# Running the FFN products of a fused attention and FFN kernel as pairs on the two column halves of the array, from the last of batch 1's transposes to the last kv

## Chip, cores, metric

One core of a Trainium2 chip. The metric is the device time of the core in microseconds, median of several executions. The record marks each execution as fast or slow (slow ones show a lower granted TensorE clock).

## The reference, cut to what matters

```python
def _attn_ref(q, k, v, g_norm):                  # 8 batches, 8 heads, 576 tokens, head size 64
    kv  = np.einsum('bhsd,bhse->bhde', k, v)     # 64 x 64 per head
    out = np.einsum('bhsd,bhde->bhse', q, kv)
    rms = np.sqrt(np.mean(out * out, axis=-1, keepdims=True) + 1e-06)
    return (out / rms * g_norm)

def _moe_ref(x, w_a, w_b, w_out):                # x: 4608 tokens x 512; d_ff 1536
    return ((x @ w_a) * (x @ w_b)) @ w_out
```

The attention's output, heads side by side, is the x of the FFN.

## The kernel before

TensorE does FFN products nearly all of the time, in nine strips of 512 tokens. The attention of the next batches is slipped in between. Three kinds of products divide the array differently:

- FFN products use all of it, 128 rows and 128 columns (128\*128 in the profile).
- `kv` gives each of two heads a column half (128\*64, or 96\*64 for the first batches), so two products run side by side. The transposes `qtr` do the same.
- `tx`, the token products of batches 2 to 7, give each head a row half (64\*128).

```python
    def product(o, lhsT, rhs, halves=False, **kw):
        for r in (slice(0, D), slice(D, 2 * D)) if halves else (slice(0, 2 * D),):
            nc.tensor.matmul(o[r], lhsT=lhsT[:, r], rhs=rhs, **kw)

        def kv(self, p, o):                       # class Attn
            ...
            for c, n in enumerate(rows):
                for j in range(2):
                    nc.tensor.matmul(
                        o[j * D : (j + 1) * D, :],
                        lhsT=kk[0:n, 2 * p + j, c, :],
                        rhs=vv[0:n, 2 * p + j, c, :],
                        start=(c == 0), stop=(c == len(rows) - 1))

        def tx(self, lent):                       # class Attn
            ...
                        r = slice(j * D, (j + 1) * D)
                        nc.tensor.matmul(
                            P[:, i, c0 + p * D : c0 + (p + 1) * D],
                            lhsT=self.qT[r, p, t0 : t0 + 128], rhs=self.kvs[r, p, :],
                            start=True, stop=True)

        def mm(self, w, kcs):                     # class Unit: one of 12 column blocks of d_ff
            t0 = self.s * STRIP
            for kc in kcs:
                nc.tensor.matmul(
                    self.a if w is wa_t else self.b,
                    lhsT=w[:, kc, self.fc * 128 : (self.fc + 1) * 128],
                    rhs=xt[:, kc, t0 : t0 + STRIP],
                    start=(kc == KORD[0]), stop=(kc == KORD[-1]))

    pieces = [(1, h1), (1, h2), (2, h1), (2, h2), (3, h1), (3, h2)]
    for n, (g, fcs) in enumerate(pieces):         # end of strip 0, with batch 1's attention
        halves = 0 < n < NP                       # NP = 4
        o_mm(0, g, O, fcs, halves=halves)         # six output products
        ...
        if n < NP:
            A.qtr(n, 2)
            A.kv1(n, 2)
        ...
    def slot(A, s, n):                            # called between the units of strip s
        k0, x0 = {1: (5, 6.5), 2: (1, 2.5), 3: (4, 5.5), 4: (0, 0.5), 5: (4, 5.5), 6: (0, 0.5)}[s]
        if n == k0 and s in (1, 2, 3, 5):
            two = [A] if s < 3 else [A, Attn(s + 2)]
            for i, a in enumerate(two):
                for p in range(NP):
                    a.kv(p, kb[:, i, p, :])       # 40 products a batch
            ...
        m = n - x0
        if m == 0:
            A.tx(ab_bank())                       # 40 products
```

So already before, pieces 1 to 3, which alternate with transposes and kv, were done in halves. The rest of the FFN was not.

Of the kernel before, what the change touches and what calls it, by code (L numbers as in the profile page):

```python
# [15 lines left out]
def kernel(  # L16
# [11 lines left out]
    nc = tc.nc  # L28

    B, H, S, D = q.shape  # L30
    d_model = H * D
# [4 lines left out]
    NP = H // 2  # L36
    HF = S // 2
    STRIP = 512
# [10 lines left out]
    def sb(shape, dt, name):  # L49
        return pool.tile(shape, dt, name=name, tag=name)  # L50
# [20 lines left out]
    xt = sb([128, KC, n_tok], BF16, "xt")  # L71
    abt = [[sb([128, STRIP], BF16, f"ab{i}_{f}") for f in range(FC)] for i in range(2)]
    a_sb = [sb([128, STRIP], BF16, f"asb{i}") for i in range(4)]
    sq = [sb([128, 2, HF], BF16, f"sq{i}") for i in range(3)]
# [16 lines left out]
    ones = sb([128, 128], BF16, "ones")  # L91
# [16 lines left out]
    P = psum.tile([128, 8, STRIP], FP32, name="P", tag="P")  # L108
    O = 3
# [44 lines left out]
        nc.sync.dma_start_transpose(qT[b % 2], qs_d[b])  # L154


    def product(o, lhsT, rhs, halves=False, **kw):
        for r in (slice(0, D), slice(D, 2 * D)) if halves else (slice(0, 2 * D),):
            nc.tensor.matmul(o[r], lhsT=lhsT[:, r], rhs=rhs, **kw)  # L159


    class Attn:
# [59 lines left out]
        def psq(self, p, i0):  # L222
            nc.scalar.activation(sq[p % 3], P[:, i0 : i0 + 2, 0:HF], AF.Square)

        def pss(self, p, i0, hs=(0, 1), halves=False):
            for h in hs:
                product(
                    P[:, i0 + h, 0:HF], ones, sq[p % 3][:, h, :], halves, start=True, stop=True
                )
            h0, h1 = hs[0], hs[-1] + 1  # L230
            nc.scalar.activation(  # L231
                rs[p % 3][:, h0:h1, :],
                P[:, i0 + h0 : i0 + h1, 0:HF],
                AF.Abs_reciprocal_sqrt,
                bias=eps_t,
            )
# [11 lines left out]
                )  # L248


        def x(self, p, i0, halves=False):
            for h in range(2):
                product(
                    P[:, i0 + h, 0:HF],
                    kvb[:, p, :],
                    self.qT[:, p, h * HF : (h + 1) * HF],
                    halves,
                    start=True,
                    stop=True,
                )  # L260
# [86 lines left out]
    class Unit:  # L347
        n = 0
# [6 lines left out]
        def mm(self, w, kcs):  # L355
            t0 = self.s * STRIP
            for kc in kcs:
                nc.tensor.matmul(  # L358
                    self.a if w is wa_t else self.b,
                    lhsT=w[:, kc, self.fc * 128 : (self.fc + 1) * 128],  # L360
                    rhs=xt[:, kc, t0 : t0 + STRIP],
                    start=(kc == KORD[0]),
                    stop=(kc == KORD[-1]),
                )
# [19 lines left out]
    def ab_bank():  # L384
        ab_banks.append(ab_banks.pop(0))
        return ab_banks[-1]
# [23 lines left out]

    n_o = [0]

    def o_mm(s, g, i, fcs, e0=0, e1=d_model, halves=False):
        for fc in fcs:
            product(
                P[:, i, e0:e1],
                abt[s % 2][fc][:, g * 128 : (g + 1) * 128],
                wo_t[:, fc, e0:e1],
                halves,
                start=(fc == 0),  # L420
                stop=(fc == FC - 1),
            )

    def o_out(s, g, i):
        n = n_o[0]
        n_o[0] += 1
        t = o_sb[n % 4]
        if n % 2:
            nc.scalar.copy(t, P[:, i, :])  # L429
        else:  # L430
            nc.vector.tensor_copy(t, P[:, i, :])  # L431
        store(s * STRIP + g * 128, t, 0, d_model)

    def ffn_o(s, g, i=O, between=None):
        o_mm(s, g, i, range(FC // 2))
        if between:
            between()
        o_mm(s, g, i, range(FC // 2, FC))
        o_out(s, g, i)
# [46 lines left out]
    X, SS = (4, 0), 6  # L486


    A = Attn(0)
# [14 lines left out]
    for c in range(EC):  # L504
        nc.tensor.matmul(
            P[:, SS, 0 : 2 * D],
            lhsT=kc0[:, c, :],
            rhs=vc[:, c, :],
            start=(c == 0),
            stop=(c == EC - 1),  # L510
        )
    for j in range(2):
        r = slice(j * D, (j + 1) * D)
# [7 lines left out]
    for p in range(1, NP):  # L521
        i = X[p % 2]
# [44 lines left out]
    A = Attn(1)  # L567
# [6 lines left out]
    pieces = [(1, h1), (1, h2), (2, h1), (2, h2), (3, h1), (3, h2)]  # L574
    for n, (g, fcs) in enumerate(pieces):

        halves = 0 < n < NP
        o_mm(0, g, O, fcs, halves=halves)
        if fcs is h2:
            o_out(0, g, O)  # L580
        if 0 <= n - 2 < NP:
            A.pss(n - 2, SS, halves=halves)
            A.pst(n - 2, X[n % 2])
        if 0 <= n - 1 < NP:
            A.x(n - 1, X[(n - 1) % 2], halves)
            A.psq(n - 1, X[(n - 1) % 2])
        if n < NP:
            A.qtr(n, 2)
            A.kv1(n, 2)
            A.kv_out(n, P[:, 2, STRIP - D :])  # L590
            A.qtr_out(n, 2)
# [9 lines left out]
    def slot(A, s, n):  # L601

        kb = P[:, 7, :].rearrange("q (b p e) -> q b p e", b=2, e=D)
        if s == 1:
            k0, xs = 5, (6.5, 8, 9.5, 11, 12.5)
        else:
            k0, x0 = {2: (2, 3.5), 3: (4, 5.5), 4: (0, 1.5), 5: (4, 5.5), 6: (0, 1.5)}[s]
            xs = tuple(x0 + x for x in (0, 1.5, 2.5, 4, 5))

        k0, x0 = {1: (5, 6.5), 2: (1, 2.5), 3: (4, 5.5), 4: (0, 0.5), 5: (4, 5.5), 6: (0, 0.5)}[s]  # L610
        if n == k0 and s in (1, 2, 3, 5):
            two = [A] if s < 3 else [A, Attn(s + 2)]
            for i, a in enumerate(two):
                for p in range(NP):
                    a.kv(p, kb[:, i, p, :])
            for i, a in enumerate(two):
                (nc.scalar.copy if i else nc.vector.tensor_copy)(a.kvs, kb[:, i])
        m = n - x0
        if m == 0:
            A.tx(ab_bank())  # L620
        for c in range(LC + 1):
            if m == 1.5 * c:
                A.tsq(c)
            if m == (1, 2, 4, 5, 7)[c]:
                A.tss(c)
            if m == (1, 2, 4, 5, 7)[c] + 0.5:
                A.trs(c)
            if m == (1, 2, 4, 5, 7)[c] + 1.5:
                A.txt(c)

    for s in range(1, N_STRIP - 1):
        b = s + 1
        A = Attn(b) if b < B else None
        for n in range(FC + 4):
            amid = (lambda n=n: slot(A, s, n - 0.5)) if A else None
            if n >= FC:
                ffn_o(s, n - FC, ab_bank() if n % 2 else O, amid)
            elif s > 1 or n > 1:
                ffn_ab(s, n, amid)
            if A:  # L640
                slot(A, s, n)

            if s == 1 and n == 3:
                load_late(3)
            if b + 1 < B and n == (12, 4, 8, 5, 8)[s - 1]:
                transpose_q(b + 1)
            if b + 2 < B and n == (14, 10, 14, 8)[s - 1]:
                load_late(b + 2)
# [12 lines left out]
    for i, copy, eng in ((6, nc.vector.tensor_copy, nc.sync), (7, nc.scalar.copy, nc.scalar)):  # L661
        e0 = hw + (i - 6) * qw
# [33 lines left out]
```

## Time and profile before

| | before |
|---|---|
| time, median (range) of the first 3 runs | 313.35 us (313.3 to 313.46) |
| span of the profile | 311.5 us |
| TensorE busy | 306.4 us, 98%, 2067 products recorded |
| full products of 512 columns, start to start | 215.8 ns |
| kv blocks between FFN products (128\*64) | 4: strips 1, 2, 3, 5 |
| tx blocks (64\*128) | 6: strips 1 to 6 |

Busy time is the union of intervals, so a pair that runs side by side counts once. A product's length (379 ns) is a latency. The pace is the distance between starts, which the timeline gives through the start of each next group. The lines themselves stand in the prediction.

### The profile page before, as it was taken

The page shows a single profiled execution, that of the slowest core. Times are in us where ns is not written, and L with a number is a line of the kernel's source. Part 1 is how long each engine was busy: PE and PEld are TensorE (multiplying, and loading weights), DVE is VectorE, ACT ScalarE, POOL GpSimd, SP SyncE. Part 2 cuts the span into 40 slices and gives each one's busy share as a digit, 9 for nine tenths or more (in the row PEclk, how much of TensorE's full clock was granted, in tenths as well). Part 3 has the DMA queues.
Part 4 walks back from the last instruction along what each step waited for, and adds up shares of the span by engine and source line. Part 5 has one row for each costly group of instructions (what it writes and reads, how often), then busy time and mean ns, then how long its engine had stood idle before and what let it go on. Part 6 is the DMA issues. An engine that isn't in the chain of part 4 may idle for free.

```text
span 311.5 us, 5288 instructions
## 1 busy us (share of the span) xinstructions
PE 306.4 (98%) x2067; PEld 145.7 (47%) x2067; DVE 140.7 (45%) x235; ACT 117.0 (38%) x231; POOL 101.2 (32%) x123
## 2 busy tenths in 40 slices
PE   8999999999999999999999999999999999999996
PEld 3444474444454444544444445444444444444444
DVE  4544335458238603484386123752783134213421
ACT  3643255354255313561554033632651233123310
POOL 8944991193274640043646300221240000000000
PEclk9999999999999999999999999999999999999999
DMA  8999999999799699046997980073021200030012
GB/s 180 197 196 199 200 189 161 223 133 165 169 172 177 106 198 168 2 89 126 172 185 109 185 167 2 19 160 109 20 51 42 103 1 0 36 100 1 0 36 101
DMA packets 94398, 36.21 MB, mean 116 GB/s; under 512 B 64934, under 2 KB 89894, under 8 KB 94374
## 3 DMA queue, kind: packets, MB, share of 16 engines
q0 software_dynamic: 59120, 18.44, 54.3%
q1 hardware_dynamic: 34786, 16.93, 23.8%
q10 hardware_dynamic: 468, 0.51, 0.6%
q8 instruction: 16, 0.26, 0.4%
q14 instruction: 8, 0.07, 0.1%
HBM read 37.78 MB, written 12.98 MB: 163 GB/s over the span
## 4 chain that ended last, share of the span: by engine, by line
PE 86%; DMA 7%; POOL 5%; issue 1%; ACT 0%; POOLq 0%
PE P L358 54%; PE P L159 29%; DMA wb_t<-in_moe_w_b_dram 6%; DMA vt<-in_v_dram 2%; PE P L176 2%; PE P L292 1%; POOL qt L119 1%; POOL wo_t L134 1%; POOL kt L119 1%; POOL vt L119 1%; POOL wb_t L477 0%; POOL wa_t L477 0%; POOL wa_t L130 0%; PE P L200 0%; POOL ident masks.py:199 0%
## 5 line engine op out<-in xcount | busy, mean ns | idle before, releaser
L376 DVE TENSOR_TENSOR ab<-P,asb 128x512 bf16<-128x512 f32 x108 | 74.5, 691 | 103.5 <-PE P L358 100.1
L358 PE MATMUL P<-xt,wa_t 128*128 128x512 bf16 x432 | 111.5, 379 | 0.1
L358 PE MATMUL P<-xt,wb_t 128*128 128x512 bf16 x432 | 111.3, 379 | 0.0
L372 ACT CAST asb<-P 128x512 bf16<-128x512 f32 x108 | 63.1, 586 | 90.0 <-PE P L358 90.0
L159 PE MATMUL P<-wo_t,ab 128*128 128x512 bf16 (+3 forms) x474 | 95.7, 368 | 0.0
L159 PEld LDWEIGHTS <-ab 128*128 128x128 bf16 (+1 forms) x474 | 44.0, 99 | 48.3
L358 PEld LDWEIGHTS <-wa_t 128*128 128x128 bf16 x432 | 41.8, 98 | 50.3 <-issue 0.6
L358 PEld LDWEIGHTS <-wb_t 128*128 128x128 bf16 x432 | 41.8, 98 | 49.8
L329 POOL TENSOR_TENSOR sqt<-rst,g_all 128x512 f32<-128x512 f32 (+1 forms) x24 | 25.0, 1043 | 84.7 <-ACT rst L322 84.7
L429 ACT COPY osb<-P 128x512 f32<-128x512 f32 x17 | 10.0, 586 | 70.2 <-PE P L159 65.6
L431 DVE COPY osb<-P 128x512 f32<-128x512 f32 x18 | 12.5, 692 | 44.9 <-PE P L159 44.9
L142 POOL DMA_DIRECT2D qs<-in_q_dram x12 | 19.8, 1654 | 0.7 <-issue 0.3
L313 DVE TENSOR_REDUCE sst<-sqt 128x8 f32<-128x512 f32 (+1 forms) x24 | 16.3, 680 | 1.7 <-ACT sqt L309 1.5
L338 DVE TENSOR_TENSOR qv<-P,sqt 128x512 bf16<-128x512 f32 x18 | 12.3, 681 | 0.0
L329 POOL TENSOR_TENSOR k_x<-rst,g_all 128x512 f32<-128x512 f32 x6 | 6.3, 1043 | 18.0 <-ACT rst L322 18.0
L322 ACT ACTIVATE rst<-sst,eps_t 128x8 f32<-128x8 f32 (+1 forms) x30 | 9.0, 300 | 7.0 <-DVE sst L313 6.8
L309 ACT ACTIVATE sqt<-P 128x512 f32<-128x512 f32 x18 | 10.5, 585 | 0.1
L241 DVE SCALAR_TENSOR_TENSOR xt<-P,g_col,rs 128x288 bf16<-128x288 f32 x16 | 7.5, 512 | 5.2 <-ACT rs L231 5.2
L134 POOL DMA_DIRECT2D wo_t<-in_moe_w_out_dram x12 | 6.4, 530 | 6.7 <-DMA wb_t<-in_moe_w_b_dram 3.1
L444 PE MATMUL P<-zeros 128*128 128x512 bf16 x17 | 6.6, 529 | 1.2 <-DVE eps_t L461 1.2
L231 ACT ACTIVATE rs<-P,eps_t 128x576 f32<-128x576 f32 (+1 forms) x9 | 6.1, 689 | 3.8 <-PE P L159 3.5
L139 POOL COPY gate<-qT 1x1 bf16<-1x1 bf16 x5 | 0.9, 176 | 17.3 <-DMA qT<-qs 17.2
(72 smaller groups left out, 130.8 us busy)
## 6 DMA issues: line engine op xcount, KB each, us to landing
out_dram<-osb SPq DMA_DIRECT2D x23, 256.0 KB, 2.0
qs<-in_q_dram POOLq DMA_DIRECT2D x12, 288.0 KB, 6.9
ktl<-in_k_dram POOLq DMA_DIRECT2D x6, 512.0 KB, 8.7
vtl<-in_v_dram POOLq DMA_DIRECT2D x6, 512.0 KB, 11.0
out_dram<-osb SPq DMA_DIRECT2D x13, 128.0 KB, 2.4
wo_t<-in_moe_w_out_dram POOLq DMA_DIRECT2D x12, 128.0 KB, 6.0
wa_t<-in_moe_w_a_dram POOLq DMA_DIRECT2D x5, 256.0 KB, 9.2
wb_t<-in_moe_w_b_dram POOLq DMA_DIRECT2D x5, 256.0 KB, 9.8
```

Of the source, the lines that this page charges most:

```text
L134: nc.gpsimd.dma_start(out=wo_t[:, i, :], in_=wo_v[:, i, :])
L142: nc.gpsimd.dma_start(out=d[:, hs, :], in_=q[b, hs].rearrange("h t d -> t h d"))
L159: nc.tensor.matmul(o[r], lhsT=lhsT[:, r], rhs=rhs, **kw)
L309: nc.scalar.activation(sqt[c % 3][r], self.by_head(c)[r], AF.Square)
L313: nc.vector.reduce_sum(sst[c % 3][r], sqt[c % 3][r].rearrange("t j p d -> t (j p) d"), axis=mybir.AxisListType.X,)
L329: nc.gpsimd.tensor_mul(sqt[c % 3][r].rearrange("t j p d -> t (j p) d"), rst[c % 3][r].unsqueeze(2).to_broadcast([n, H, D]), g_all[r].unsqu ...
L338: nc.vector.tensor_mul(t[r].rearrange("t (p j) d -> t j p d", j=2), self.by_head(c)[r], sqt[c % 3][r])
L358: nc.tensor.matmul(self.a if w is wa_t else self.b, lhsT=w[:, kc, self.fc * 128 : (self.fc + 1) * 128], rhs=xt[:, kc, t0 : t0 + STRIP], st ...
L372: nc.scalar.copy(self.t, self.a)
L376: nc.vector.tensor_mul(abt[self.s % 2][self.fc], self.b, self.t)
L429: nc.scalar.copy(t, P[:, i, :])
L431: nc.vector.tensor_copy(t, P[:, i, :])
```

## The change

Its intent: kv and FFN products use the same division of the array, so that nothing has to be switched around a kv. The flag becomes a state that stays on from piece 1 until just before the last kv (strip 5), and the products of `Unit.mm` go through `product` as well.

```diff
+    halves = [False]
-    def product(o, lhsT, rhs, halves=False, **kw):
-        for r in (slice(0, D), slice(D, 2 * D)) if halves else (slice(0, 2 * D),):
+    def product(o, lhsT, rhs, **kw):
+        for r in (slice(0, D), slice(D, 2 * D)) if halves[0] else (slice(0, 2 * D),):
             nc.tensor.matmul(o[r], lhsT=lhsT[:, r], rhs=rhs, **kw)
 ...                                     # pss, x, o_mm lose their own argument
         def mm(self, w, kcs):
             for kc in kcs:
-                nc.tensor.matmul(
+                product(
 ...
-        halves = 0 < n < NP
-        o_mm(0, g, O, fcs, halves=halves)
+        halves[0] = n > 0
+        o_mm(0, g, O, fcs)
 ...
         if n == k0 and s in (1, 2, 3, 5):
+            halves[0] = s < 5
```

More of the change, by code (lines that the diff above doesn't have):

```diff
@@ L223, in psq, with pss @@
             nc.scalar.activation(sq[p % 3], P[:, i0 : i0 + 2, 0:HF], AF.Square)
-        def pss(self, p, i0, hs=(0, 1), halves=False):
+        def pss(self, p, i0, hs=(0, 1)):
             for h in hs:
                 product(
-                    P[:, i0 + h, 0:HF], ones, sq[p % 3][:, h, :], halves, start=True, stop=True
+                    P[:, i0 + h, 0:HF], ones, sq[p % 3][:, h, :], start=True, stop=True
                 )
@@ L248, in pst, with x @@
                 )
-        def x(self, p, i0, halves=False):
+        def x(self, p, i0):
             for h in range(2):
@@ L256, in x @@
                     self.qT[:, p, h * HF : (h + 1) * HF],
-                    halves,
                     start=True,
@@ L357, in mm @@
             for kc in kcs:
-                nc.tensor.matmul(
+                product(
                     self.a if w is wa_t else self.b,
-                    lhsT=w[:, kc, self.fc * 128 : (self.fc + 1) * 128],
-                    rhs=xt[:, kc, t0 : t0 + STRIP],
+                    w[:, kc, self.fc * 128 : (self.fc + 1) * 128],
+                    xt[:, kc, t0 : t0 + STRIP],
                     start=(kc == KORD[0]),
@@ L411, with o_mm @@
     n_o = [0]
-    def o_mm(s, g, i, fcs, e0=0, e1=d_model, halves=False):
+    def o_mm(s, g, i, fcs, e0=0, e1=d_model):
         for fc in fcs:
@@ L418, in o_mm @@
                 wo_t[:, fc, e0:e1],
-                halves,
                 start=(fc == 0),
@@ L581 @@
         if 0 <= n - 2 < NP:
-            A.pss(n - 2, SS, halves=halves)
+            A.pss(n - 2, SS)
             A.pst(n - 2, X[n % 2])
         if 0 <= n - 1 < NP:
-            A.x(n - 1, X[(n - 1) % 2], halves)
+            A.x(n - 1, X[(n - 1) % 2])
             A.psq(n - 1, X[(n - 1) % 2])
```

## The prediction

> **What bounds the kernel now.** I read the page first: the line of busy times, then the chain that ended last.
>
> ```profile
> PE 306.4 (98%) x2067; PEld 145.7 (47%) x2067; DVE 140.7 (45%) x235; ACT 117.0 (38%) x231; POOL 101.2 (32%) x123
> PE 86%; DMA 7%; POOL 5%; issue 1%; ACT 0%; POOLq 0%
> ```
>
> TensorE is busy all the time, and after the loads of the start it is the whole chain. Busy is no proof of full pace, so I looked at its waits: the view of waits holds three for PE, 1.2, 0.4 and 0.2 us, all of the first 17 us. After that the end is set by how fast TensorE gets through its list, and only what changes that pace matters. Next, the matmul groups with shapes kept apart:
>
> ```profile
> L358 PE MATMUL P<-xt,wa_t 128*128 128x512 bf16 x432 | 111.5, 379 | 0.1
> L358 PE MATMUL P<-xt,wb_t 128*128 128x512 bf16 x432 | 111.3, 379 | 0.0
> L159 PE MATMUL P<-wo_t,ab 128*128 128x512 bf16 x402 | 88.6, 379 | 0.0
> L176 PE MATMUL P<-vtl,ktl 128*64 128x64 bf16 x240 | 4.6, 197 | 0.0
> L292 PE MATMUL P<-kvs,qT 64*128 64x64 bf16 x240 | 4.5, 190 | 0.0
> L159 PE MATMUL P<-wo_t,ab 128*64 128x512 bf16 x36 | 4.5, 379 | 0.0
> ```
>
> 128\*128 is the part of the array that a product uses (rows\*columns). Some 1,270 full products of 512 columns are the kernel. Their 379 ns is a latency; start to start the trace gives a mean of 215.8 ns. The kernel before already has 36 half products (128\*64), the kind that the change multiplies, so both cost and gain can be read from it. The timeline of TensorE around pieces 1 to 3 (start, length to the last end, group):
>
> ```profile
> 39.85 1.49 PE L159 MATMUL P<-wo_t,ab 128*64 128x512 bf16 x12
> 41.15 0.44 PE L159 MATMUL P<-qT,kvb 128*64 128x288 bf16 x4
> ...
> 44.14 0.38 PE L176 MATMUL P<-vt,kt 96*64 96x64 bf16 x12
> 44.33 1.49 PE L159 MATMUL P<-wo_t,ab 128*64 128x512 bf16 x12
> ...
> 46.80 1.47 PE L159 MATMUL P<-wo_t,ab 128*128 128x512 bf16 x6
> 48.10 0.41 PE L159 MATMUL P<-sq,ones 128*128 128x288 bf16 x2
> ```
>
> Twelve halves take from 39.85 to 41.15, 1.30 us; the six full products of the same work take from 46.80 to 48.10, also 1.30 us. A half pair costs what one full product costs. The timeline around the kv and the token products (tx) of strip 1:
>
> ```profile
> 59.63 1.03 PE L358 MATMUL P<-xt,wb_t 128*128 128x512 bf16 x4
> 60.59 0.82 PE L176 MATMUL P<-vtl,ktl 128*64 128x64 bf16 x40
> 61.34 1.04 PE L358 MATMUL P<-xt,wa_t 128*128 128x512 bf16 x4
> 62.22 1.03 PE L358 MATMUL P<-xt,wb_t 128*128 128x512 bf16 x4
> 63.08 1.03 PE L358 MATMUL P<-xt,wa_t 128*128 128x512 bf16 x4
> 64.04 0.76 PE L292 MATMUL P<-kvs,qT 64*128 64x64 bf16 x40
> 64.73 1.04 PE L358 MATMUL P<-xt,wb_t 128*128 128x512 bf16 x4
> ```
>
> Four full products from 59.63 end their pace at 60.49 (4 x 0.2158), but kv starts at 60.59: 0.10 us are lost at this change of the array's division. It is lost again at 61.34, at 64.04 and at 64.73, but not between 62.22 and 63.08 (0.86 = 4 x 0.2158).
>
> **What the Trainium skill says.** "TensorEngine Tiling (Array Packing)", Key Properties: changing the tiling mode, not just the tile, drains TensorE, and different tiles load weights and multiply independently. The trace agrees with both: about 0.10 us at each change of mode, and two halves in the time of one full product. The same page, Feature Incompatibilities, says that column tiling excludes Fast Weight Load. The load groups agree in direction (128\*64 takes 110 ns, 128\*128 takes 98 ns, for half the columns), but loads lie under the products. "TensorE: Matmul & The Clock Gate", Wait — 56ns, not 53.3ns?, gives N / 2.4 + 2.5 ns from start to start, 215.8 for N = 512; the 215.8 of the trace agrees. If the fixed 2.5 ns were paid per half, a pair would take 218.3; the half pairs of the trace start 215.5 ns apart inside a block, so it isn't.
>
> **The change part by part.**
>
> 1. *More instructions.* The instruction order of both kernels shows 4133 against 5401 rows on TensorE, a weight load and a product each: 634 further products. By hand: 12 + 6 in pieces 4 and 5 (output, norm and x products), 16 in the first units of strip 1, 80 + 48 for the rest of strip 1, 3 x 144 for strips 2 to 4, 40 for the units 0 to 4 of strip 5; 634. The order on VectorE, ScalarE, GpSimd and SyncE is the same. Price: 634 pairs x (215.5 - 215.8 ns), about 0; I count 0 and leave up to -0.2 us in the range.
>
> 2. *Switches removed.* Strips 1, 2, 3 and 5 hold a kv block, and before each has a switch in and one out. In, per instruction of the trace: 309 ns from the last full product to the first of kv instead of 216 (+93), and the second pair comes after 53 instead of the usual 32 ns (+21): 114 ns. Out: from the first of the last kv pair to the full product 131 instead of 32 (+99), and the second full product after 227 (+11): 110 ns. The chain shows the +11 and the drain together: 12 full products after a kv take 2.70 there, and 2.59 where no switch precedes them.
>
> ```profile
> 61.41 2.70 PE P L358 x12
> 149.13 2.59 PE P L358 x12
> ```
>
> Now halves hold from piece 1 until the last kv (strip 5). Removed: the four switches in, the switches out of strips 1, 2 and 3, and the one out after piece 3 (46.80); the one after strip 5's kv stays. 4 x 114 + 4 x 110 = 896 ns.
>
> 3. *Seams in their place.* Between kv and halves the pieces show 3 ns (44.33), then a first pair of 221 instead of 216. About 10 ns each way: 4 x 10 = 40 ns back.
>
> 4. *The tx blocks stay switched.* tx uses 64\*128, neither mode, so strips 1 to 4 still drain twice each, now from and to 128\*64. Before, in is 312 against 216 (+96), out 123 against 29 (+94) and +11. From columns halved the trace has only other cases (transposes 96\*64 to 64\*64 near 10 us: 136 against 39, +97), so a drain costs about the same. But of a half pair the second starts 3 to 28 ns after the first, so a drain may end later by that, and the first load without the fast path is longer (+21 against +11). Estimate 4 x 25 = 100 ns lost.
>
> Sum: -896 + 40 + 100 = -756 ns. All of it lies on the chain, as TensorE waits for nothing here. 313.35 - 0.75 = 312.6 us.
>
> **The rivals.**
>
> - *Halves are slower in long streams than in blocks of 12.* Double instruction traffic, double moving reads, no fast weight load. With the 2.5 ns per product of the skill, 634 x 2.5 = 1.6 us, net 314.2; at 10 ns it would be +6.3, net 318.9. Against it: 215.5 ns within all three blocks, while DMA was at its busiest, and kv blocks put a pair with two loads through every 32 ns, so loads and issue have room for seven times that rate. The instruction queue moved only 0.26 MB, and would move about 0.34 (x 5401 / 4133).
> - *tx switches get dearer when rows and columns change both.* Eight switches at 0.1 us more would eat the gain, 313.4. For it: no such switch is in the trace. Against: the five kinds there all cost 93 to 99 ns before refilling, whichever sides change.
> - *A load takes the place of the switch.* In strip 3 the second batch's values land at 124.16, and its products begin at about 124.97. TensorE would come some 0.6 us earlier, so the margin shrinks to 0.2; the issues (from 107.45) are held by earlier work that moves forward too. At worst 0.2 us lost, 312.8. In strip 1 the last values land at 59.32, 1.27 us ahead.
> - *Evictions.* A bank is full up to 28 ns later. PE waits for no eviction before, and VectorE and ScalarE are under half busy: nothing.
>
> **Range and chances.** The centre is 312.6. Full recovery with faster pairs gives 312.2; dearer tx switches or 1 ns per pair, up to 313.4. I take 312.1 to 313.5. The 2% lines are at 307.1 and 319.6: nothing removed reaches the first, and the second needs 10 ns a pair. Faster 0.01, within 2% 0.97, slower 0.02.
>
> **What would show it.** 2701 products; half pairs start 215 to 216 ns apart in long strips (by groups of four products: 0.86 us); kv blocks of strips 1 to 3 without the 0.10 us before and after; 0.10 us still at every tx and after the kv of strip 5; no new PE wait; span shorter by 0.6 to 0.9 us. I am wrong if pairs in long streams take over 217 ns, if PE's tx gaps exceed 0.15 us, or if a DMA releases kv.

## The result, and the profile after

The changed kernel took 312.68 us (312.43 to 313.0, 4 runs), the kernel before 313.38 us in the same rounds. The ratio is 0.9978, 95% interval 0.9961 to 0.9996. Ratios here are the mean time of one kernel's fast runs over that of the other's of the same rounds, so not quite the ratio of the medians. The interval lies below 1 as a whole. The gain is 0.70 us where 0.75 was forecast.

That agreement hides something. First the page of the changed kernel:

```profile
PE 304.3 (98%) x2684; PEld 157.6 (51%) x2701; DVE 140.6 (45%) x235; ACT 117.0 (38%) x231; POOL 101.3 (33%) x123
PE 79%; DMA 12%; POOL 7%; issue 1%; ACT 0%; POOLq 0%
```

There are 2701 weight loads, as predicted (17 records of their products are missing). But DMA's share of the chain rose from 7% to 12%. The timeline of TensorE after piece 3 and in strip 2 (start, length to the last end, group):

```profile
46.42 0.38 PE L178 MATMUL P<-vt,kt 96*64 96x64 bf16 x12
46.61 1.49 PE L161 MATMUL P<-wo_t,ab 128*64 128x512 bf16 x12
47.91 0.44 PE L161 MATMUL P<-sq,ones 128*64 128x288 bf16 x4
```

```profile
85.34 1.03 PE L161 MATMUL P<-xt,wb_t 128*64 128x512 bf16 x8
86.20 0.80 PE L178 MATMUL P<-vtl,ktl 128*64 128x64 bf16 x40
86.83 1.03 PE L161 MATMUL P<-xt,wa_t 128*64 128x512 bf16 x8
...
89.53 0.76 PE L293 MATMUL P<-kvs,qT 64*128 64x64 bf16 x40
90.21 1.05 PE L161 MATMUL P<-xt,wb_t 128*64 128x512 bf16 x8
```

The way out after piece 3 is gone: the FFN products start 0.19 us after the first kv product (46.61 - 46.42), where the kernel before took 0.31 us (46.80 - 46.49). In strip 2 everything is as intended. Eight halves take 86.20 - 85.34 = 0.86 us, the pace of four full products, and kv follows without a gap. kv takes 86.83 - 86.20 = 0.63 us, where the kernel before needed 61.34 - 60.49 = 0.85 for the same 40 products with a switch on either side. Strip 1 is different:

```profile
59.45 1.06 PE L161 MATMUL P<-xt,wb_t 128*64 128x512 bf16 x8
60.32 1.07 PE L178 MATMUL P<-vtl,ktl 128*64 128x64 bf16 x40
61.19 1.06 PE L161 MATMUL P<-xt,wa_t 128*64 128x512 bf16 x8
```

Here the 40 products take 61.19 - 60.32 = 0.87 us instead of 0.63. The chain that ended last (start, length, what) says why:

```profile
47.20 13.45 DMA vtl<-in_v_dram
60.69 0.69 PE P L178 x32
61.38 2.59 PE P L161 x24
```

After eight products kv waits for batch 2's last values, which land at 60.65 us. The kernel before had them at 59.32. So the wait that the prediction had placed in strip 3 came in strip 1, and took about 0.25 us (a gap of 251 ns where 29 is usual, and some 20 ns to get back into step).

The time of a run also scatters with its first 46 us, which are the same program in most of these kernels. In the profiles, piece 3's kv starts anywhere from 46.4 to 46.8 us without any change ahead of it (the three kernels with a changed start, at the end, are left aside). That is half of the gain. Therefore I use, beside the times, **the stretch**: from the last kv product of piece 3 to the start of the very last product of TensorE, as the trace has them. Two profiles of the kernel before agree on it to 1 ns (261.583 and 261.584 us). In the changed kernel it is shorter by 578 ns, with the wait in it.

### The profile page after: what moved, and what is told of

It reads as the page before. It is cut to its first block, busy times and chain, and to the rows that moved or that the text cites. A ratio compares the mean times of both kernels' runs of the same rounds, so it can differ in the third digit from the quotient of the medians.

```text
span 310.8 us, 6542 instructions
## 1 busy us (share of the span) xinstructions
PE 304.3 (98%) x2684; PEld 157.6 (51%) x2701; DVE 140.6 (45%) x235; ACT 117.0 (38%) x231; POOL 101.3 (33%) x123
## 4 chain that ended last, share of the span: by engine, by line
PE 79%; DMA 12%; POOL 7%; issue 1%; ACT 0%; POOLq 0%
PE P L161 77%; DMA wb_t<-in_moe_w_b_dram 6%; DMA vtl<-in_v_dram 4%; DMA wo_t<-in_moe_w_out_dram 2%; PE P L293 1%; PE P L178 1%; POOL vt L119 1%; POOL qt L119 1%; POOL qs L142 1%; POOL kt L119 1%; POOL wa_t L477 0%; POOL wb_t L477 0%; POOL wo_t L134 0%; POOL ktl L145 0%; POOL vtl L145 0%
## 5 line engine op out<-in xcount | busy, mean ns | idle before, releaser
L161 PE MATMUL P<-xt,wb_t 128*64 128x512 bf16 (+1 forms) x641 | 111.4, 379 | 0.2
L161 PE MATMUL P<-xt,wa_t 128*64 128x512 bf16 (+1 forms) x636 | 111.0, 379 | 0.6 <-issue 0.2
L161 PE MATMUL P<-wo_t,ab 128*64 128x512 bf16 (+3 forms) x673 | 95.5, 371 | 0.3
L161 PEld LDWEIGHTS <-ab 128*64 128x64 bf16 (+1 forms) x678 | 47.5, 106 | 45.0
L161 PEld LDWEIGHTS <-wa_t 128*64 128x64 bf16 (+1 forms) x644 | 46.0, 106 | 46.2 <-issue 0.6
L161 PEld LDWEIGHTS <-wb_t 128*64 128x64 bf16 (+1 forms) x644 | 45.8, 106 | 45.8
L444 PE MATMUL P<-zeros 128*128 128x512 bf16 x16 | 5.8, 510 | 1.2 <-DVE eps_t L461 1.2
```

## The experiments

All use the kernel before or the changed kernel with one edit, and all gave correct results. They ran in four groups; the time of before is that of the same group.

| kernel | time, us (before) | stretch against before, ns |
|---|---|---|
| changed, first profile | 312.68 (313.38) | -578 |
| after_again | 312.56 (313.32) | -725 |
| kv_later | 312.59 (313.32) | -824 |
| to_end | 312.50 (313.32) | -883 |
| price | 313.56 (313.32) | +226 |
| split_before | 314.48 (313.39) | +897 |
| split_after | 312.49 (313.39) | -821 |
| split_n | 315.02 (313.39) | +1584 |
| end_later | 312.21 (313.39) | -898 |
| shift_after | 313.22 (313.28) | -822 |
| shift_before | 313.90 (313.28) | -2 |
| before_again | 313.42 (313.28) | +1 |
| fetch_full | 313.72 (313.30) | -2 |

**Theories.** Mine: pairs cost nothing, each switch costs 0.11 us, and a load that varies eats part of the gain. Rivals: the halves are themselves faster or slower in long streams; kv is slow for another reason than the switch; the halves slow the DMAs.

### after_again: the changed kernel once more

> The changed kernel again. Median 312.5 to 312.8, spread wider than before's (some 0.5 us). Theory of the varying load wait: TensorE's wait inside the kv block of strip 1 (0.22 us in the first profile) is another length or gone in this profile, and the time differs accordingly. Rival, halves slow the DMA queues: the queues' shares are again 56% and 25% (before: 54.3% and 23.8%), with the landing of batch 2's last values after 60.4 again.

Measured: 312.56 us (312.44 to 312.96), ratio 0.9974 (0.9962 to 0.9987). The wait was there again but shorter: a gap of 105 ns inside kv, and a stretch of -725 instead of -578 ns. The wait thus varies from run to run. The DMA shares were 55.8% and 25.7% again, and the values landed at 60.61. So the later landing is no chance of one profile, and the rival about the DMAs stayed alive.

### kv_later: strip 1's kv half a unit later

```diff
-        k0, x0 = {1: (5, 6.5), 2: (1, 2.5), ...
+        k0, x0 = {1: (5.5, 6.5), 2: (1, 2.5), ...
```

> The changed kernel with strip 1's kv block half a unit (0.86 us) later. If the wait for batch 2's values is what keeps the gain under 0.80 us and makes it scatter: 312.5 to 312.6, spread back to 0.2 us or less, no gap inside the kv block of strip 1. If the scatter has another cause: the same 312.4 to 313.0 as the changed kernel.

```profile
60.38 1.06 PE L161 MATMUL P<-xt,wa_t 128*64 128x512 bf16 x8
61.24 0.82 PE L178 MATMUL P<-vtl,ktl 128*64 128x64 bf16 x40
61.87 1.06 PE L161 MATMUL P<-xt,wb_t 128*64 128x512 bf16 x8
```

kv takes 0.63 us in strip 1 too, the wait is gone, and the stretch is -824 ns. The times do not show it: 312.59 us (312.44 to 312.88) against the 312.56 of the changed kernel. The half of the expectation that spoke of the scatter failed: 0.44 us is left of it, so most of it does not come from this wait. The start is the likely place of what is left; the runs without a profile cannot show it.

### price: halves where no kv is

Halves only in strip 7 and in strip 8 but its last group, on top of the kernel before (pieces 1 to 3 as before).

```diff
     for s in range(1, N_STRIP - 1):
+        halves[0] = s == 7
```

> The kernel before with halves in strip 7 and all of strip 8 but its last group: 276 further pairs, no switch removed, one in and one out added. Pairs free: 0.22 us slower than before, 313.6. A pair dearer by 2.5 ns: 0.9 us slower, 314.3. Halves themselves faster (the rival source of the gain, 1.1 ns a pair or more to explain 0.7 us over 634): no slower than before or faster.

```profile
246.48 1.05 PE L161 MATMUL P<-xt,wa_t 128*64 128x512 bf16 x8
247.37 1.03 PE L161 MATMUL P<-xt,wb_t 128*64 128x512 bf16 x8
248.23 1.03 PE L161 MATMUL P<-xt,wa_t 128*64 128x512 bf16 x8
```

Once in step, eight halves take 248.23 - 247.37 = 0.86 us, as four full products do. Measured: 313.56 us, ratio 1.0004 (0.9992 to 1.0017), which by itself does not resolve so small a change; stretch +226 ns. That is one switch in and one out (114 + 110 = 224) and 276 pairs for nothing. Both rivals about the pace of halves fall. Neither 2.5 ns more nor 1.1 ns less per pair is there; 2 ns over 276 pairs are left.

### split_before and split_after: twice as many kv blocks

Each kv block is cut in two, with half a unit (four products) between the parts; all the other work is the same.

```diff
             for i, a in enumerate(two):
-                for p in range(NP):
+                for p in range(NP // 2):
                     a.kv(p, kb[:, i, p, :])
+        if n == k0 + 0.5 and s in (1, 2, 3, 5):
+            for i, a in enumerate(two):
+                for p in range(NP // 2, NP):
+                    a.kv(p, kb[:, i, p, :])
```

> The kernel before with each kv block cut in two, four full products of the strip between the parts: the same work and instructions, four more blocks, so eight more switches. My theory (0.11 us a switch): 8 x 0.112 = 0.9 us slower than before, 314.2. Rival, kv is slow for another cause than the switch (small products): 313.3 as before.

> The same cut in the changed kernel, where the parts of strips 1 to 3 lie between halves; strip 5 keeps halves until its second part. My theory: no switch is added, 312.5 to 312.8 as the changed kernel, and the 0.9 us between the two kernels before becomes 1.6 to 1.7 us between these. Rival (the cut itself costs): as much slower than the changed kernel as the cut kernel before is than before.

The timeline of strip 1, first of split_before, then of split_after:

```profile
60.90 0.51 PE L176 MATMUL P<-vtl,ktl 128*64 128x64 bf16 x20
61.34 1.04 PE L358 MATMUL P<-xt,wa_t 128*128 128x512 bf16 x4
62.30 0.51 PE L176 MATMUL P<-vtl,ktl 128*64 128x64 bf16 x20
```

```profile
60.48 0.51 PE L178 MATMUL P<-vtl,ktl 128*64 128x64 bf16 x20
60.80 1.06 PE L161 MATMUL P<-xt,wa_t 128*64 128x512 bf16 x8
61.66 0.51 PE L178 MATMUL P<-vtl,ktl 128*64 128x64 bf16 x20
```

With full products from one part of kv to the next: 62.30 - 60.90 = 1.40 us. With halves: 61.66 - 60.48 = 1.18. The difference, 0.22 us, is one switch in and one out. The eight added switches lengthened the stretch by 897 ns, where 8 x 112 = 896 were expected. In the changed kernel the cut cost nothing (-821; the wait was absent, as the values had landed at 60.33 us, before this kv began at 60.48). The times are 314.48 and 312.49: 1.99 us apart, more than the 1.6 to 1.7 expected and the 1.72 of the stretches (897 + 821). In the profiles, 0.21 us of it lies ahead of the stretch: piece 3's kv starts at 46.80 and 46.59. That kv is slow for another reason than the switch is out.

### to_end: halves until the end

```diff
-            halves[0] = s < 5
+            halves[0] = True
```

> The changed kernel with halves kept to the end of the program (560 more pairs). My theory (pairs free, each switch 0.11 us): one switch out less, 0.1 us faster than the changed kernel, 312.3 to 312.7 with its scatter. Rival, a pair costs 1 ns or more: 0.5 us slower than the changed kernel or worse.

Measured: 312.50 us (312.35 to 313.04), ratio 0.9972. Stretch -883: some 60 ns shorter than the -821 to -824 of the changed kernel's variants without a wait. One exit of about 110 ns was removed, but tx in strips 5 and 6 now lies between halves, at 13 ns each: 84 worked out. From strip 5 on, the trace has 79 ns less than that of kv_later; the other 16 were lost before strip 1. So the 560 further pairs show no price of their own. By the times alone the difference from the changed kernel is not resolved.

### split_n: as many instructions without halves

Each full product in the same stretch is cut into two of 256 columns on the whole array.

```diff
+        if halves[0] == 2:
+            m = rhs.shape[-1] // 2
+            for c in (slice(0, m), slice(m, 2 * m)):
+                kc = dict(start=kw["start"] and c.start == 0, stop=kw["stop"] and c.start > 0)
+                nc.tensor.matmul(o[:, c], lhsT=lhsT, rhs=rhs[:, c], **kc)
+            return
```

> The kernel before with as many instructions as the changed one, without halves of the array: in the same stretch each full product is cut into two of 256 columns on the whole array, with a weight load each. From the 109 ns of such products in strip 8: 634 x 2.6 ns = 1.6 us slower than before, 315.0. Theory of the instruction fetch (twice the instructions, so a 16 KB fetch falls at 56 to 58 us into batch 2's loads): the last values land at 60.0 to 60.7 us as in the changed kernel. Rival, halves of the array disturb the DMA writes: they land at 59.3 to 59.5 as in the kernel before.

Measured: 315.02 us, ratio 1.0055 (1.0042 to 1.0068), stretch +1584 ns, as worked out: the fixed cost per product is real when products follow each other on the same columns. It is not paid twice when they lie side by side. On the landing it told nothing: the values landed at 59.59, but the instruction fetch came at 59.7, just after them, and not inside the load. The premise of the test was not met.

### end_later: both later kv and halves to the end

> Halves to the end and strip 1's kv half a unit later, together. No wait in strip 1, one switch less: from the point after piece 3 to the end 0.94 us less than before in the trace (0.84 + 0.10); times 312.3 to 312.7, under the changed kernel by 0.1 to 0.3 us, which the scatter of the start (0.3 us) may hide.

Measured: 312.21 us (311.97 to 312.43), ratio 0.9963 (0.9950 to 0.9975), the fastest of all medians and 1.2 us under before. Its stretch is -898, 76 ns under the changed kernel's without the wait, where 116 were expected (-940 forecast); the small tx cost of strips 5 and 6 had been left out. As its measured time is further ahead of before than its stretch, some of the 1.2 us is luck of the start.

### shift_after, shift_before, before_again, fetch_full: why do the values land later?

The traces show TensorE's program being fetched by DMA, in packets of 16 KB: 16 of them (0.26 MB) in the kernel before, 21 (0.34 MB) in the changed one, so where the instructions are twice as many the packets come closer together. They show such a packet at 56.5 to 57.8 us, lasting 1.1 to 2.1 us, in all kernels with halves in strip 1 but shift_after, so in the second half of batch 2's loads. In the kernel before it came at 61.5 us, after them. The first two kernels shift the fetches by the number of warm-up products at the start; the third is the kernel before unchanged.

```diff
-    dummy(10, 0)
+    dummy(52, 0, 96)      # shift_after, in the changed kernel
+    dummy(29, 0, 176)     # shift_before, in the kernel before
+    dummy(66, 0, 76)      # fetch_full, in the kernel before
```

> The changed kernel with 52 warm-up products of 96 columns at the start in place of 10 of 512: 84 more instructions ahead, about the same time, so that the instruction fetches come 84 instructions earlier, near 53 and 64 us, and none at 57 to 58. Theory of the instruction fetch: batch 2's last values land at 59.3 to 59.6 us (given loads issued as in the other runs), though the halves are all there, and the kv block of strip 1 has no wait. Rival, halves of the array disturb the DMA writes: they land at 60.1 to 60.7 us as in the five kernels with halves. Time 312.4 to 312.7 either way, as the start scatters by 0.3 us.

> The kernel before with 29 warm-up products of 176 columns in place of 10 of 512: 38 more instructions, so that the fetch of 61.5 us comes near 57.5. Theory of the instruction fetch: batch 2's last values land at 60.0 to 60.7 us with no halves in that stretch. Rival: 59.3 to 59.6 us as in the kernel before. Time 313.3 to 313.7, for kv comes at 60.6 with its last chunk 0.1 us later, so it waits little or not.

> The kernel before as a kernel of its own, for a second profile: ratio 1.000, batch 2's last values land at 59.3 to 59.6 us, the instruction fetch near 61.5 us.

Both shifts missed their aim. In shift_after the fetch came at 55.0, still inside the load, which landed at 59.84: between the two forecasts. The moved fetches also made batch 1's values late (0.9 us of waiting near 41 us in the view of waits), hence 313.22 us, with runs from 312.19 to 313.52. In shift_before the fetch moved only to 60.8, because the 80 instructions of a kv block pass in 0.6 us, and the values landed at 59.57. Its time was 313.90, over the 313.3 to 313.7 expected, with its stretch unchanged: other waits near the start. before_again landed at 60.10, later than expected, with no fetch inside. So chance, or something not found, moves the landing as well. I then placed the fetch by counting the instructions back through the kv block:

> The kernel before with 66 warm-up products of 76 columns in place of 10 of 512: 112 more instructions, as the 38 of the try before moved the fetch only into the kv block (60.8 us). The fetch should come near 57.5 us into batch 2's loads, with full products there. Measured from the issue of the last values' load to their landing, the kernels without halves took 11.8 to 12.1 us, once 12.7, those with halves 12.7 to 13.5. Theory of the instruction fetch: 12.7 us or more. Rival, halves disturb the DMA writes: 11.8 to 12.2 us. The time may be 0.9 us over before's, since the same kind of shift made batch 1's values late in the changed kernel.

From the issue of the load of the last values to the landing, as the view of that line has it, in the kernel before, the changed kernel and fetch_full:

```profile
DMA to landing us min/median/max: 12.1/12.1/12.1
```

```profile
DMA to landing us min/median/max: 13.4/13.4/13.4
```

```profile
DMA to landing us min/median/max: 13.5/13.5/13.5
```

In fetch_full the fetch lay at 55.8 us (1.66 us long), with full products only, and the load took as long as in the changed kernel. Its time was 313.72 us (two runs): 0.42 us over before, where up to 0.9 was expected, with 0.7 us of waiting for batch 1's values. Over all profiles the load took 12.7 to 13.5 us in the eight with a fetch inside it (after 50 us; most have one more near its issue), and 11.8 to 12.1 us in five of the six without, once 12.7 (before_again). A landing as late as the changed kernel's is thus seen without halves there, in one profile.

That the two landings took the same time is not yet the same cause. The trace has sixteen counts of the load's semaphore, and the landing is the last. In the kernel before they come from 58.35 to 59.32 us. In the changed kernel twelve have come by 58.85, no later than before, and the last four come from 60.40 to 60.65, after the fetch of 57.81 to 59.52. The same gap of some 1.5 us, ending 0.75 to 0.9 us after the end of the fetch, is in after_again, split_after and end_later; without a fetch there no gap exceeds 0.5 us. In fetch_full there is no such gap: all sixteen come late, from 59.72 on (likewise in kv_later and to_end, from 59.47 and 59.14). So the fetch is the likely cause in the changed kernel, by its place in time, but no experiment isolates it there. Whether halves add something of their own is left open, as no profile has halves and no fetch inside the load. The transposing DMAs speak against much of it: from 198 to 249 us, with no loads running, their packets took 20.9 and 20.6 ns on average with halves there (to_end, end_later), and 19.7 to 20.5 in four profiles without (before, before_again, after, kv_later).

## Why the prediction was right, point by point

- *634 further pairs at no price*: shown. price adds 276 pairs for 2 ns, to_end 560 for nothing seen. Half pairs in long streams start 215 to 216 ns apart, as full products do.
- *Eight switches at 114 and 110 ns*: shown by price (+226 for one of each) and split_before (+897 for four of each).
- *Seams of 10 ns each way, 40 in all*: mis-sized. (Four entries and four exits at 10 ns would also have been 80, not 40.) The kv blocks of strips 2 and 3 gained all of their 224 ns: kv to halves takes 4 to 29 ns, and the pair after it comes 3 ns late. It is nearly 0.
- *tx blocks, 25 ns dearer each, 100 in all*: right in sign, too large. Into tx it is 315 ns from the first half of the last pair, where it was 312 from a full product; out of it it is 120 instead of 123, with a second pair after 240 instead of 227. Together about 13 ns a block, 52 in all. (The prediction's +94 for the way out of tx before should be +97: it set 123 ns, from the later product of a pair, against 29, from the earlier; like with like it is 126 against 29.) The rival of dearer tx switches did not happen.
- *The sum*: -896 + 52 = -844, and 21 ns of one short wait for ScalarE before the last norm product of batch 1 (208 ns where 186 is usual) give -823. Measured without the load wait: -821 to -824. The forecast of -756 was 67 ns too careful.
- *"A load takes the place of the switch"*: it happened, but not where it was placed. Of the prediction's signs of being wrong, "if a DMA releases kv" thus came true, and its "no new PE wait" did not hold. The prediction looked at strip 3 and set strip 1 aside because its values landed 1.27 us ahead. It overlooked that the landing itself would move, although it worked out the larger instruction traffic (0.34 MB, and 0.34 were measured). By the stretch the wait cost 0.25 us in the first profile (824 - 578) and 0.10 in the second (824 - 725). The times gained 0.70 and 0.76 us in those two groups, with the scatter of the start in them.
- The predicted 312.6 us is thus close to the 312.68 partly because two errors cancel: a gross gain that was set too low and a wait that was set at zero.

## What to carry to other kernels

When small column-tiled products are scattered among full ones, let the full ones run as pairs on the same column halves: pairs have the pace of the full product, and each avoided change of mode saves about 0.11 us. It pays by the number of switches, not by the amount of work, so count the switches first. More instructions may not be free for the rest of the core: the instruction fetches become denser, and loads with one inside landed later here (12.7 to 13.5 us against mostly 11.8 to 12.1), so look at the margin of each load with its landing allowed to move, and make the consumer later where it is thin.

## What the Trainium skill lacked or had wrong

- "TensorEngine Tiling (Array Packing)", Key Properties, says that changing the tiling mode drains TensorE, but gives no size. Here the drain was 93 to 99 ns in every change between 128\*128, 128\*64 and 64\*128, with some 10 to 24 ns more before the second product or pair; 114 ns into kv and 110 ns out of it. It hardly depends on which sides of the array change. The page also does not say that a product of full width can be split into two column halves for nothing: 215 to 216 ns a pair against 215.8.
- "TensorE: Matmul & The Clock Gate", Part 3, What overlaps and what doesn't, lets weight loads overlap running products only where the row group differs. Here loads for the same 128 rows start 2 ns after a running product of the same columns did, and the pairs keep 215 to 216 ns. (Its Part 2, and the text above that list in Part 3, allow for a background weight buffer, which agrees.)
- "Runtime: NRT & Kernel Launch", Instruction fetch mechanics, calls the cost of crossing a 16 KiB block mostly hidden. For TensorE this agrees: its pairs kept 215 to 216 ns. It does not speak of other DMAs: the load with a fetch of 0.9 to 2.1 us inside it took 12.7 to 13.5 us to land, and without one 11.8 to 12.1, once 12.7.
